# Moving normalised rows and inverse-softmax products from VectorE to GpSimd, with a new pace table, in a four-layer attention and MLP kernel

## The chip, the cores and the metric

The kernel runs on one core of a Trainium2 chip. The metric is the device time of one execution in microseconds (us). The core has TensorE (PE, matrix products), VectorE (DVE), ScalarE (ACT), GpSimd (POOL) and SyncE (SP, which issues the DMAs here). The profile adds PEld, TensorE's weight loads.

## The reference

Two layers of attention and two of a squared-ReLU MLP follow each other, on 2048 rows of 448 columns in bfloat16. Both attention layers use the same weights, and so do both MLPs.

```python
def A(x, wqkv, wo):                  # 16 heads of 28
    q, k, v = split(x @ wqkv)
    p = softmax(q @ k.T * 28 ** -0.5)
    return (p @ v).merge_heads() @ wo

def B(x, w1, b1, w2, b2):            # 448 -> 1792 -> 448
    r = maximum(x @ w1 + b1, 0)
    return (r * r) @ w2 + b2

x = x + A(layernorm(x)); x = x + B(layernorm(x), ...)
x = x + A(layernorm(x)); x = x + B(layernorm(x), ...)
```

`layernorm` is (x - mean) / sqrt(var + 1e-5), without weights.

## The kernel before

**Who orders the work.** The order of instructions on every engine is written by a planner in the kernel file when the program is built. Each piece of work is an `Op` with an engine, an assumed duration, what it depends on and which buffers it takes and gives back. Streams of Ops have priorities; `Planner.run` takes the Op that can start earliest, and by priority among equals. `Planner.earliest` works that time out from the ends of the dependencies (plus a latency of each engine, and `lat` of the Op) and from the engine's clock. An Op with `port=True` is on VectorE or GpSimd and uses SBUF on both sides; the planner doesn't start it inside such an Op of the other engine. Only the order is kept from the plan: on the chip each engine runs its list in order and waits on semaphores.

**Attention.** A score bank is 128 keys by 512 columns (two blocks of 128 keys for 256 queries of one head; for the last row blocks four for 128). A step computes three banks in one PSUM tile `sc` (`s_stream`, L924), and there are two such tiles. ScalarE takes the exponential of three banks in one instruction of 1536 columns (`e_stream`, L954), or of two banks in one of 1024 columns. In the second case VectorE does the third bank with an approximation of 2^x from bits, in four instructions: `take` (L1002, VectorE, reads PSUM and frees the bank), `part` (L1019, GpSimd, an add and a multiply on SBUF), `bend` (L1025, VectorE, a square) and `close` (L1032, VectorE, adds and writes bits). The function `apart` decides for each step whether VectorE takes a bank. One of its conditions is a bound on VectorE's planned backlog, read from the table `PACE` at the place of the step in the whole run:

```python
if max(0.0, pl.clock["DVE"] - now) + left[0] > PACE[i * len(PACE) // len(units)]:
    return None
```

The probabilities times V (`p_stream`, L1095) go into PSUM tiles `oT`, with the softmax sums in an extra column of each head. `p_stream` copies them to SBUF (L1121, L1123). For each pair of head groups `norm_pair` sends the sums to DRAM and back by three kinds of DMA on SyncE's queue (`dn`, `scr`, `rec`; L1198, L1209, L1217) with a reciprocal in between (L1203), so that their inverses lie spread over the rows, and multiplies (`mul`, L1222, 128x512, two float32 inputs and a bfloat16 output `oTn`). The last few row blocks use `norm_turn` with transposes on VectorE in its place (L1164 to L1180).

**The dense parts.** `chain` takes one block of 256 rows (128 at the end): the projection `wo` and the addition to `x_sb` (L655, L1231), statistics (L509, L514), `layernorm`, w1 with relu (L1289) and square (L1296), w2 and the addition, and in the first layer pair the statistics, `layernorm` and `qkv` for the second. `layernorm` takes the inverse root of the variance on GpSimd (L536, L537), normalises each 128 rows of 448 columns (`norm`, L619, into `xn`), transposes on TensorE (L559) and copies back (L571). In the opening the first three blocks are marked `early`. The very last block is done by `ends_last`.

**Fillers.** While the scores' share of TensorE is low, score matmuls are issued again (`again` in `s_stream`, into the same place), and `heat` issues products that nobody reads (L1516).

Of the kernel before, what the change touches and what calls it, by code (L numbers as in the profile page):

```python
# [13 lines left out]
ALU = mybir.AluOpType  # L14
# [12 lines left out]
GY = 0.65  # L27
# [48 lines left out]
PACE = (3.6, 2.2, 2.2, 1.8, 1.8, 1.8, 1.8, 3.0, 0.3, 0.9, 2.2, 2.2, 2.2, 1.4, 1.4, 1.4, 1.4, 1.4, 1.4, 2.2, 2.2, 2.2, 2.2, 1.4, 3.0, 3.0, 2.2, 2.2, 2.2, 1.8, 4.5, 4.5, 2.6, 2.6, 3.0, 3.0, 3.0, 3.6, 3.0, 1.4, 3.0, 4.5, 4.5, 4.5, 1.4, 1.4, 0.9, 1.4, 0.3, 1.4, 1.4, 1.4, 2.2, 2.2, 1.8, 1.8, 1.8, 1.8, 2.6, 2.6, 1.8, 1.8, 0.3, 6.0)  # L76
# [47 lines left out]
class Op:  # L124
    __slots__ = ("eng", "dur", "fn", "deps", "acq", "rel", "mode", "sets", "start", "end", "res", "turn", "ready", "lat", "need", "got", "more", "room", "port")

    def __init__(self, eng, dur, fn, deps=(), acq=None, rel=None, mode="full", sets=(), lat=0.0, need=1, port=False):
        self.eng = eng if isinstance(eng, tuple) else (eng,)
        self.dur, self.fn, self.deps, self.mode, self.lat = dur, fn, deps, mode, lat
        self.rel = rel if isinstance(rel, list) else ([] if rel is None else [rel])  # L130
        self.acq = acq if isinstance(acq, tuple) or callable(acq) else (() if acq is None else (acq,))
        self.sets = sets if isinstance(sets, list) else ([sets] if sets else [])
        self.start = self.end = self.res = self.turn = None
        self.need, self.got, self.more, self.port = need, [], 0.0, port
# [5 lines left out]
class Planner:  # L140
# [22 lines left out]
    def earliest(self, o):  # L163
        t = 0.0
        for d in o.deps:
            if not isinstance(d, Op):
                d = self.tok.get(d)
            if d is None or d.end is None:
                return None, None
            same = d.eng[0] == o.eng[0] and len(o.eng) == 1  # L170
            t = max(t, d.end + d.lat + ((0.03 if same else 0.10) if d.eng[0] == "DVE" else
                                (0.0 if same and d.eng[0] != "DMA" else LAT[d.eng[0]])))
# [68 lines left out]
def kernel(  # L241
# [12 lines left out]
    nc = tc.nc  # L254
# [265 lines left out]
    def layernorm(t0, nt, deps_of, early=False, mv=None, place=None, x_in=None, parts=False):  # L520
# [9 lines left out]
        for a, b in [(0, 1), (1, 2)] if single else [(0, nt)]:  # L530
# [9 lines left out]
            pl.spawn(EV, iter([rs]))  # L540
        box = {}
# [68 lines left out]
        for p0 in range(0, nt, wide):  # L610
# [4 lines left out]
            for j in js:  # L615
                xn = xns[2 * (own.turn % 2) + j % 2]

                def norm(e, j=j, xn=xn):
                    nc.vector.tensor_scalar(out=xn[:, 0:D], in0=x_sb[:, t0 + j, :],  # L619
                                            scalar1=mv[0][:, j, 0:1], scalar2=ln[j],  # L620
                                            op0=ALU.subtract, op1=ALU.mult)
                nm = Op("DVE", 0.39, norm, deps=[rss[j], *([] if x_in is None else [x_in])], sets=[("n", t0, j)] if early else (), port=True)
                yield nm
                xs.append((xn, nm))
# [387 lines left out]
    def a_rest(gi, c, box, unit):  # L1012
# [7 lines left out]
        y = Op("POOL", GY, part, deps=[c, ("p", gi)] if own else [c], acq=None if own else lambda: pd_free(unit), port=True)  # L1020
# [13 lines left out]
        o = Op("DVE", 0.683, close, deps=[h], rel=c, sets=("x", gi), port=True)  # L1034
# [151 lines left out]
    def norm_pair(l, qb, g, pair):  # L1186
# [34 lines left out]
        def mul(e):  # L1221
            nc.vector.tensor_tensor(out=oTn_of[l, qb][0][:, g:g + 2, 0:n], in0=both,  # L1222
                                    in1=box["r"][:, :, 0:n], op=ALU.mult)
        m = Op("DVE", 0.13 + 2 * n / 930, mul, deps=[r, oTn_of[l, qb][1]], rel=pair["own"], port=True)
# [9 lines left out]
    def chain(l, qb):  # L1234
# [43 lines left out]
        for f0 in range(0, NFC, pack):  # L1278
# [11 lines left out]
            def square(e, b=b, w=w, f0=f0):  # L1290
                r = b["r"][:, 0:w].rearrange("p (f q) -> p f q", q=n)
                b["h"] = h = hidden(f0 // pack)
                if e == "ACT":
# [4 lines left out]
            def then(o, b=b, square=square):  # L1298
                aside = not s_left and (l, qb) == (1, len(blocks[1]) - 2)
                b["s"] = Op("ACT" if aside else "DVE", 0.5 if aside else 0.42, square, deps=[o], rel=o, port=True)  # L1300
# [267 lines left out]
```

## Time and profile before

| | |
|---|---|
| median of 3 runs | 847.54 us (846.21 to 848.14) |
| profiled execution | 845.42 us |
| its span on the core | 843.6 us |
| mean granted clock of TensorE | 0.994 |
| busy: PE, DVE, ACT, POOL | 806.6, 783.8, 821.3, 225.3 us |
| exponentials L954 (1536 and 1024 columns) | 422 and 261 |
| banks of VectorE (L1002) | 260 |

The span runs from the first to the last instruction of the core; the time of the execution has 1.8 us more around it. Durations in the profile are those of single instructions, which overlap at their ends, so a busy time is less than count times mean. A "group by form" shows a line of the source, the engine, the operation, tiles and shapes, then the count, the busy time and mean duration, and the idle time of the engine before these instructions with what ended it. The table by stretches has the busy time of each engine with its count of instructions, then TensorE's granted clock and the DMA's share and rate. "A <- B: t, n, m" among the waits says that the engine waited in A for B, t us in all, n times, at most m. An answer on a line gives its count and the minimum, median and maximum duration in ns.

### The profile page before, as it was taken

Reading aid. Unit: us, or ns where it says so; the run is one execution under the profiler, and the core shown is the slowest. Engines: PE = TensorE matmul, PEld = TensorE weight load, DVE = VectorE, ACT = ScalarE, POOL = GpSimd, SP = SyncE. Lnnn points to the kernel's source line nnn. Section 1 sums busy time; section 2 is a strip of 40 time slices with the busy share of each in tenths; the row PEclk is TensorE's granted clock in tenths of the full one; section 3 lists DMA queues with packets and bytes.
Section 4 is the critical chain, followed back from the end, with each engine's and each line's share of the span. In section 5 each row is a group of like instructions: output and inputs, shape, how many; then the busy total and the mean of one; then the engine's idle time right before and its main releaser. Section 6 shows DMA issues by size and latency. Waiting matters only on the chain.

```text
span 843.6 us, 28341 instructions
## 1 busy us (share of the span) xinstructions
PE 806.6 (96%) x12255; PEld 428.6 (51%) x12255; DVE 783.8 (93%) x1610; ACT 821.3 (97%) x700; POOL 225.3 (27%) x354
## 2 busy tenths in 40 slices
PE   8999999999999999999999999989999999999997
PEld 4455545554545455455445444534554545545565
DVE  7999989999989999999999999989989999999955
ACT  8998999999999999999999999989999999999994
POOL 3222322223222233222332333332222222232300
PEclk9999999999999999999999999989999999999999
DMA  9200000000000000000000000011000000000000
GB/s 251 68 3 2 25 20 15 16 15 15 15 3 16 15 15 16 7 11 15 2 2 3 2 2 3 11 30 32 18 23 21 20 26 15 14 25 16 17 11 18
DMA packets 32365, 17.98 MB, mean 21 GB/s; under 512 B 17833, under 2 KB 31787, under 8 KB 32240
## 3 DMA queue, kind: packets, MB, share of 16 engines
q1 hardware_dynamic: 32240, 16.18, 6.9%
q8 instruction: 95, 1.56, 0.8%
q14 instruction: 30, 0.25, 0.1%
HBM read 13.88 MB, written 2.07 MB: 19 GB/s over the span
## 4 chain that ended last, share of the span: by engine, by line
PE 44%; DVE 27%; ACT 22%; issue 5%; DMA 1%; POOL 0%; SPq 0%; ACTq 0%; DVEq 0%
ACT pt L954 22%; PE mt L655 18%; PE sc L924 15%; PE oT L1095 8%; DVE v_w L1002 3%; DVE pt L1032 2%; DVE r L1289 2%; DVE V_sb L1032 2%; DVE K_sb L1002 2%; DVE pt L1025 2%; DVE V_sb L1025 1%; PE mt L1516 1%; DVE xn L619 1%; DVE oTn L1222 1%; DVE Q_sb L674 1%
## 5 line engine op out<-in xcount | busy, mean ns | idle before, releaser
L954 ACT ACTIVATE pt<-sc 128x1536 bf16<-128x1536 f32 (+1 forms) x683 | 810.0, 1377 | 9.1 <-PE sc L924 8.0
L924 PE MATMUL sc<-Q_sb,K_sb 32*128 32x256 bf16 (+1 forms) x5258 | 308.6, 267 | 22.3 <-ACT pt L954 17.1
L924 PEld LDWEIGHTS <-K_sb 32*128 32x128 bf16 x5258 | 131.1, 92 | 202.5 <-issue 157.5
L1095 PE MATMUL oT<-pt,V_sb 128*32 128x256 bf16 (+1 forms) x4008 | 154.2, 270 | 1.2 <-DVE pt L1032 0.7
L1002 DVE TENSOR_SCALAR v_w<-sc 128x512 f32<-128x512 f32 x187 | 127.4, 683 | 10.7 <-PE sc L924 9.9
L655 PE MATMUL mt<-xnT,w 128*128 128x256 bf16 (+1 forms) x888 | 118.6, 271 | 0.9 <-DVE xnT L571 0.4
L1095 PEld LDWEIGHTS <-V_sb 128*32 128x32 bf16 x4352 | 91.4, 96 | 50.9 <-issue 47.7
L655 PEld LDWEIGHTS <-w 128*128 128x128 bf16 x896 | 74.9, 98 | 35.6 <-issue 27.3
L1019 POOL TENSOR_SCALAR V_sb<-v_w 128x512 bf16<-128x512 uint16 x74 | 54.2, 733 | 131.1 <-DVE v_w L1002 130.3
L1289 DVE TENSOR_SCALAR r<-mt 128x512 bf16<-128x512 f32 x108 | 73.9, 684 | 6.3 <-PE mt L655 5.9
L1019 POOL TENSOR_SCALAR pt<-v_w 128x512 bf16<-128x512 uint16 x69 | 46.2, 670 | 114.0 <-DVE v_w L1002 91.4
L655 PE MATMUL mt<-w,V_sb 128*128 128x448 bf16 (+1 forms) x288 | 70.5, 349 | 0.0
L1002 DVE TENSOR_SCALAR K_sb<-sc 128x512 f32<-128x512 f32 x73 | 49.8, 683 | 4.6 <-PE sc L924 4.5
L1032 DVE SCALAR_TENSOR_TENSOR V_sb<-v_w,V_sb 128x512 int16<-128x512 f32 x74 | 51.5, 698 | 0.1
L1032 DVE SCALAR_TENSOR_TENSOR pt<-v_w,pt 128x512 int16<-128x512 f32 x69 | 47.7, 694 | 0.1
L1231 DVE TENSOR_TENSOR x_sb<-x_sb,mt 128x448 bf16<-128x448 bf16 x62 | 37.9, 612 | 8.7 <-PE mt L655 8.4
L1025 DVE TENSOR_TENSOR pt<-pt 128x512 bf16<-128x512 bf16 x99 | 45.1, 468 | 0.7 <-POOL pt L1019 0.7
L1025 DVE TENSOR_TENSOR V_sb<-V_sb 128x512 bf16<-128x512 bf16 x89 | 41.4, 474 | 2.5 <-POOL V_sb L1019 2.5
L1019 POOL TENSOR_SCALAR pt<-K_sb 128x512 bf16<-128x512 uint16 x30 | 21.6, 719 | 71.9 <-DVE K_sb L1002 51.5
L509 DVE BATCH_NORM_STATS2 st<-x_sb 128x6 f32<-128x448 bf16 x63 | 38.7, 616 | 1.2 <-DMA x_sb<-in_A_x_dram 0.7
L1516 PE MATMUL mt<-xn,ident 128*128 128x448 bf16 x105 | 36.5, 364 | 0.9 <-DVE oT_sb L1123 0.3
L655 PEld LDWEIGHTS <-V_sb 128*128 128x128 bf16 x302 | 24.3, 98 | 25.2 <-issue 12.1
(143 smaller groups left out, 882.1 us busy)
## 6 DMA issues: line engine op xcount, KB each, us to landing
rec<-scr SPq DMA_DIRECT2D x54, 128.0 KB
x_sb<-in_A_x_dram SPq DMA_DIRECT2D x8, 224.0 KB
out_dram<-x_sb SPq DMA_DIRECT2D x15, 112.0 KB
w<-in_B_w_dram SPq DMA_DIRECT2D x1, 1568.0 KB
w<-in_B_w_dram SPq DMA_DIRECT2D x1, 1344.0 KB
dn<-oT_sb SPq DMA_DIRECT2D x54, 4.0 KB
V_sb<-in_A_wqkv_dram SPq DMA_DIRECT2D x4, 168.0 KB
scr<-dn SPq DMA_DIRECT2D x27, 8.0 KB
```

The source lines that it names most:

```text
L509: nc.vector.bn_stats(out=box["st"][:, :], in_=x_sb[:, t0 + j, :] if src is None else src())
L655: nc.tensor.matmul(box["t"][:, c0:c0 + n], lhsT=lhsT() if callable(lhsT) else lhsT, rhs=rhs, start=a, stop=b)
L924: nc.tensor.matmul(dst[k][:, i * nt * P:(i + 1) * nt * P], lhsT=K_sb[l][rows, g, (kb + i) * P:(kb + i + 1) * P], rhs=Q_sb[rows, g, t0 * P: ...
L954: t = nc.scalar.activation(out=pt[:, 0:n], in_=gbuf[gi]["sc"][:, 0:n], func=AF.Exp, scale=float(np.log(2.0)) * 2.0 ** -FRAC)
L1002: t = nc.vector.tensor_scalar(out=box["w"], in0=two(src), scalar1=EXP_SHIFT, scalar2=EXP_LOW, op0=ALU.add, op1=ALU.max)
L1019: nc.gpsimd.tensor_scalar(out=two(pd), in0=low, scalar1=-EXP_MID * 65536, scalar2=EXP_BEND, op0=ALU.add, op1=ALU.mult)
L1025: nc.vector.tensor_tensor(out=pd, in0=pd, in1=pd, op=ALU.mult)
L1032: nc.vector.scalar_tensor_tensor(out=two(pd.bitcast(DT.int16)), in0=box["w"], scalar=EXP_BITS, in1=two(pd), op0=ALU.add, op1=ALU.add)
L1095: nc.tensor.matmul(box["t"][DHP * hh:DHP * hh + DHP, 0:n], lhsT=V_sb[l][:, kb + i, 4 * g + hh, :], rhs=p[:, c0:c0 + n], start=begin and kb ...
L1231: nc.vector.tensor_tensor(out=x_sb[:, tb, lo:hi], in0=x_sb[:, tb, lo:hi], in1=t[:, 0:hi - lo], op=ALU.add)
L1289: nc.vector.tensor_scalar(out=r[:, 0:w], in0=t[:, 0:w], scalar1=0.0, scalar2=None, op0=ALU.max)
L1516: nc.tensor.matmul(t[:, 0:D], lhsT=ident[:, :], rhs=xns[0][:, 0:D], start=True, stop=True)
```

## The change

Four things are changed.

1. The normalisation of `layernorm` runs on GpSimd, but not in the `early` blocks. It is written as (x + (-mean)) * rstd there; the new `turned` negates the means on VectorE, one instruction of 128x2 (or 128x1) per call, into spare columns of the same small tile.
2. The product `mul` of `norm_pair` runs on GpSimd.
3. `PACE` has 128 entries in place of 64, from 1.0 to 4.0 with a mean of 2.41 (before 0.3 to 6.0, mean 2.23). Its lines are left out below.
4. Assumed durations and latencies of the planner change: `GY`, the new `YL` and `XL`, `GN` and `GM`. `earliest` keeps the dependencies' part of its result in `base`; it gives the same.

Squares on GpSimd are written in too, but switched off (`GS_ON = 0`).

```diff
-GY = 0.65
+GY = 0.617
+XL = 0.25
+YL = 0.05
+GN = 0.56
+GM = 1.3
+GS = 1.3
+GN_E = 0
+GM_ON = 1
+GS_ON = 0
+GS_STOP = 100
...
             rs = Op("POOL", 0.95, rsqrt, deps=[mv[1][b - 1]], sets=[("rs", t0 + a)] if early else (), port=True)
             rss += [rs] * (b - a)
             pl.spawn(EV, iter([rs]))
+            if not parts and (GN_E or not early):
+                def turned(e, a=a, b=b):
+                    ln["m"] = mv[0][:, 2:4, 0]
+                    nc.vector.tensor_scalar(out=ln["m"][:, a:b], in0=mv[0][:, a:b, 0], scalar1=-1.0, scalar2=None, op0=ALU.mult)
+                ng = Op("DVE", 0.07, turned, deps=[mv[1][b - 1]])
+                yield ng
...
                 def norm(e, j=j, xn=xn):
+                    if e == "POOL":
+                        nc.gpsimd.tensor_scalar(out=xn[:, 0:D], in0=x_sb[:, t0 + j, :],
+                                                scalar1=ln["m"][:, j:j + 1], scalar2=ln[j],
+                                                op0=ALU.add, op1=ALU.mult)
+                        return
                     nc.vector.tensor_scalar(out=xn[:, 0:D], in0=x_sb[:, t0 + j, :],
                                             scalar1=mv[0][:, j, 0:1], scalar2=ln[j],
                                             op0=ALU.subtract, op1=ALU.mult)
-                nm = Op("DVE", 0.39, norm, deps=[rss[j], ...
+                on = GN_E or not early
+                nm = Op("POOL" if on else "DVE", GN if on else 0.39, norm, deps=[rss[j], ...
...
-        y = Op("POOL", GY, part, deps=..., acq=..., port=True)
+        y = Op("POOL", GY, part, deps=..., acq=..., port=True, lat=YL)
...
-        o = Op("DVE", 0.683, close, deps=[h], rel=c, sets=("x", gi), port=True)
+        o = Op("DVE", 0.683, close, deps=[h], rel=c, sets=("x", gi), port=True, lat=XL)
...
         def mul(e):
-            nc.vector.tensor_tensor(out=oTn_of[l, qb][0][:, g:g + 2, 0:n], in0=both,
+            (nc.gpsimd if e == "POOL" else nc.vector).tensor_tensor(out=oTn_of[l, qb][0][:, g:g + 2, 0:n], in0=both,
                                     in1=box["r"][:, :, 0:n], op=ALU.mult)
-        m = Op("DVE", 0.13 + 2 * n / 930, mul, deps=[r, oTn_of[l, qb][1]], rel=pair["own"], port=True)
+        m = Op("POOL" if GM_ON else "DVE", GM if GM_ON else 0.13 + 2 * n / 930, mul, deps=[r, oTn_of[l, qb][1]], rel=pair["own"], port=True)
```

38 lines of the change are left out of this document (22 added, 16 removed).

## The prediction

> **What bounds the kernel now.** I read the page first, for the share of each engine:
>
> ```profile
> span 843.6 us, 28341 instructions
> PE 806.6 (96%) x12255; PEld 428.6 (51%) x12255; DVE 783.8 (93%) x1610; ACT 821.3 (97%) x700; POOL 225.3 (27%) x354
> PE 44%; DVE 27%; ACT 22%; issue 5%; DMA 1%; POOL 0%; SPq 0%; ACTq 0%; DVEq 0%
> ```
>
> Three engines are above 90%, and the chain of waits is shared among them, so shares alone don't say which one sets the time. TensorE's is the least firm: the kernel fills its gaps with repeated scores and the junk products of L1516. So I took the table by stretches, cut at the first and the last exponential (10.65 and 829.2 us), with three odd stretches beside:
>
> ```profile
> core 0: us, PE busy (x) PEld busy (x) DVE busy (x) ACT busy (x) POOL busy (x), PEclk, DMA share, GB/s
> 75.00:80.00 5.00, 4.41 (x65) 2.88 (x67) 4.74 (x11) 2.25 (x2) 0.62 (x1) 1.00 0.02 5
> 398.30:443.70 45.40, 43.47 (x651) 21.91 (x640) 44.40 (x96) 45.40 (x42) 15.64 (x25) 1.00 0.01 2
> 545.00:560.00 15.00, 13.19 (x186) 5.24 (x182) 12.34 (x27) 13.17 (x12) 4.78 (x6) 0.66 0.13 37
> 10.65:829.20 818.55, 787.46 (x12073) 416.10 (x12070) 769.50 (x1556) 810.03 (x684) 219.10 (x338) 0.99 0.07 19
> 829.20:843.60 14.40, 10.72 (x133) 7.82 (x130) 7.56 (x26) 3.08 (x7) 0.56 (x1) 1.00 0.06 18
> ```
>
> Between the first and the last exponential ScalarE is busy 810.03 of 818.55 us, 99%. That stretch is a queue of exponentials; the 14.4 us behind it are TensorE's. Then the groups by form, and ScalarE's waits:
>
> ```profile
> L954 ACT ACTIVATE pt<-sc 128x1536 bf16<-128x1536 f32 x422 | 607.8, 1541 | 4.7 <-PE sc L924 4.0 <-PE oT L1095 0.3
> L954 ACT ACTIVATE pt<-sc 128x1024 bf16<-128x1024 f32 x261 | 278.7, 1113 | 4.4 <-PE sc L924 4.0 <-ACT pt L954 0.3
> ACT pt L954 <- PE sc L924: 8.0, 12, 3.1
> L1002 DVE TENSOR_SCALAR v_w<-sc 128x512 f32<-128x512 f32 x187 | 127.4, 683 | 10.7 <-PE sc L924 9.9
> L619 DVE TENSOR_SCALAR xn<-x_sb,mv,rstd 128x448 bf16<-128x448 bf16 x63 | 26.0, 437 | 2.6 <-POOL rstd L537 2.6
> L1222 DVE TENSOR_TENSOR oTn<-oT_sb,rec 128x512 bf16<-128x512 f32 x27 | 21.8, 806 | 1.3 <-DMA rec<-scr 1.3
> ```
>
> There are 683 steps of three score banks. In 422 ScalarE takes all three, in 261 two, and VectorE takes the third (L1002). Consecutive exponentials overlap by their last 0.2 us, so the price is start to start: the median in the trace is 1.330 us for three banks and 0.904 for two. 422 x 1.330 + 261 x 0.904 = 797.2 us of the 818.6; the other 21 are small delays. A bank moved to VectorE is worth 1.330 - 0.904 = 0.426 us.
>
> **The change, part by part.** The changed program can be built, and its order of instructions counted. The steps stay 683, and now 403 are of three banks and 280 of two, so VectorE takes 279 banks in place of 260. On ScalarE: 19 x 0.426 = **-8.1 us**, on the path, as long as its delays stay what they are.
>
> What VectorE gains and pays, by busy time over count. Each bank costs it L1002 0.682, L1025 0.468 and L1032 0.699: 19 x 1.849 = +35.1. Away go 57 of the 63 normalisations (57 x 0.413 = -23.5; the six of the opening stay) and all 28 products (27 x 0.807 + 0.4 = -22.2). The negated mean is new, 29 of at most 0.15 us (the 128x1 rows L1404 and L1414 take 0.153 and 0.148): +4.3. One relu and one square go to ScalarE behind its last exponential: -1.1. Sum -7.4: VectorE is lent more than it pays.
>
> GpSimd gets 19 more L1019 (0.707 each, +13.4), the 57 normalisations and the 28 products. No row shows the last two there. L1019 has one input of 512 columns and takes 0.617 us when alone and up to 1.256:
>
> ```profile
> L1019 POOL TENSOR_SCALAR pt<-K_sb x30: 617/618/1256, 145.1 to 765.2; 128x512 bf16<-128x512 uint16 x30
> L1222 DVE TENSOR_TENSOR oTn<-oT_sb,rec x28: 416/684/1100, 101.6 to 804.3; 128x512 bf16<-128x512 f32 x27, 128x256 bf16<-128x256 f32 x1
> ```
>
> A normalisation of 448 columns lies between 0.617 x 448/512 = 0.54 and 1.26 us; I take 0.6, by the row that is alone. A product reads two inputs: between 0.62 and twice that behind a wait of 0.68, 1.9; I take 1.2. That is 57 x 0.6 + 28 x 1.2 + 13.4 = 81 us, and GpSimd goes from 225 to about 307, 37%: its own room is ample. Each result comes 0.2 to 0.5 us later than VectorE's. Transposes wait for the one, the projection for the other; TensorE sat 0.9 us in all behind L619 and 0.5 behind L1222, with other work in between, so this is covered; uncovered, 57 x 0.2 + 28 x 0.5 would be 25 us. The product now waits for its broadcast (rec) at the head of GpSimd's queue, with L1019 behind it, and VectorE's L1025 behind those. On VectorE that wait came once, 1.3 us: the transfers land in time. SyncE's issues keep their order but for neighbours in the opening, at nothing.
>
> The two engines disturb each other, though. Of the 260 L1025, 166 ran beside no GpSimd instruction, at 0.415 us on average, and 94 did, at 0.568; for L1032 173 at 0.680 and 87 at 0.743; for L1222 14 at 0.663 and 14 at 0.921; with L619 and L1296 this costs VectorE 28.4 us. 6.4 of it leave with the moved work. GpSimd's undisturbed work on SBUF goes from 260 x 0.617 + 35 = 196 us to 279 x 0.617 + 35 + 34 + 34 = 275, so the remaining 22 grow by 275/196 and by 6% for more VectorE instructions, to 33. VectorE's gain of 7.4 turns into a loss of 2 to 4. Within the exponentials it then has about 772 us of work in 810, 95%. The stretch 398.3 to 443.7 held 98% with ScalarE never idle, so it still fits. I charge **+1 us** of delays (from 0 to +8).
>
> Here a page speaks against the change. By the Trainium skill's page "SBUF — State Buffer", section "SBUF: two separate sides", the port pair that VectorE and GpSimd share is locked for a whole instruction, and the later one waits it out. The longest cases agree: an L1025 of 0.834 us is 0.415 and 0.42 more. By that rule the 664 two-input instructions of VectorE, 0.82 per us, meet the new 34 + 34 us on GpSimd 56 times, and wait half a product (0.6) or half a normalisation (0.3): 25 us in place of the 11 by the rows. VectorE is then at 786 us, 97%, just below what that stretch held; the delays go to their upper end, 8, and the sum to 850.0. That counts with the first rival.
>
> Two places differ in TensorE's order. From 75.4 to 79.8 us it has 52 matmuls for projections and outputs between two score tiles, held by VectorE's evictions; ScalarE waits 3.1 us. In the changed order the longest such run has 28 (some 2 us of work), with three of that kind: **-2.0** (between 0 and -3.1). The tail gets longer. After the last scores the program before has 24 matmuls of w1 with 128 columns, 15 of w2 with 448 and 32 of outputs; the changed one has 40, 33 and 64. At the tail's rates (0.056, 0.189 and 0.013 us): 0.9 + 3.4 + 0.4 = 4.7, and the last addition has 448 columns in place of 128, +0.26. TensorE is busy 12.6 of the 13.5 us there, so little idle time is left to take it: **+4.6** (from +3.8 to +5.5). In the main stretch this work lay under the exponentials, so nothing comes back for it.
>
> Sum: -8.1 + 1.0 - 2.0 + 4.6 = **-4.5 us**. The profiled execution took 845.42 (span 843.6 and 1.8 around it), 2.1 below the median of 847.54; the difference carries over: **843.0 us**.
>
> **Rivals.** *VectorE falls behind through the shared access to SBUF*, slower. It counts from the point where VectorE's work passes 98% of the shortened stretch, 0.98 x 811 = 795, that is 23 us more disturbance than I counted. By the growth above, 49% of the 558 L1025 and L1032 will be hit (181 of 520 now). A hit costs them 0.110 on average now; at the 0.258 that L1222 pays, the disturbance is 73 us and not 33: 772 + 40 = 812 needs 828 us at 98%, 17 over: 843.0 - 1 + 17 = 859. At 0.225 a hit it would be 851, and below 0.19 VectorE keeps up. For it: VectorE stands above 95% in the stretch shown, and the instructions that GpSimd newly gets are as long as VectorE's own, or longer. Against: the mean price of a hit now is less than half of that, and ScalarE waited 8 us in all for late scores. Chance 0.24.
>
> *Nothing measurable*: the tail takes 5.5, the stall at 80 us comes back elsewhere and one more stretch at a low clock (545 to 560, granted 0.66, some 2.5 us lost) appears, which fewer repeated scores (5116 L924 in place of 5258, of which 4352 are needed) make likelier: -8.1 + 5.5 + 2.5 = 0, 847.5. Chance 0.13.
>
> *The small delays shrink too*: the low-clock stretch doesn't come back (-2.5) and the new pace leaves VectorE less crowded where ScalarE now waits, -4 more: 836.5 to 839. Chance 0.1. That the change doesn't do what it says is out: the order has 57 normalisations and 28 products on GpSimd and 280 narrow exponentials.
>
> **How the numbers follow.** The forecast has 0.53 and spans 839.5 to 845.8 by its bounds. A measurement here tells 0.2%, 1.7 us, from no change. Faster: 0.53 + 0.1 = 0.63; same 0.13; slower 0.24. The range takes in the third rival but for its end and the nearer half of the first: 836.5 to 852, leaving out some 0.04 below and 0.13 above.
>
> **What would show it.** Right: L954 near 802 us with 403 and 280; an idle time before it of 6 to 10 us; VectorE at 93 to 95%; the last exponential ends near 819, and 18 to 19 us follow. Wrong: L1025 and L1032 far above 0.47 and 0.70; a product over 1.9 us on GpSimd; ScalarE's waits for L924 well above 8 us; or a tail like before's.

## The result, and the profile after

The changed kernel takes 856.6 us (854.97 to 857.06, 4 runs), the kernel before 847.83 us beside it on the same chip (846.21 to 848.14, 4 runs): a ratio of 1.0104 [1.0085, 1.0123]. It is 1% slower; 843.0 was forecast, and 836.5 to 852 as range. The profiled execution took 856.41 us.

The profile's page:

```profile
span 854.4 us, 28257 instructions
PE 806.0 (94%) x12126; PEld 423.8 (50%) x12126; DVE 795.5 (93%) x1609; ACT 817.1 (96%) x702; POOL 324.4 (38%) x458
DVE 40%; PE 36%; ACT 15%; issue 7%; POOL 1%; DMA 0%; POOLq 0%; ACTq 0%; DVEq 0%
```

In the last line, the shares of the chain that ended last, VectorE has risen from 27% to 40%; its busy share has not moved from 93%. The table by stretches, cut again at the first and the last exponential, with one stretch inside (columns as in the prediction's table):

```profile
10.77:835.11 824.34, 781.87 (x11896) 407.82 (x11893) 779.73 (x1552) 804.82 (x683) 318.51 (x443) 0.99 0.07 18
835.11:854.40 19.29, 15.56 (x181) 11.18 (x178) 9.08 (x29) 4.11 (x9) 0.56 (x1) 0.97 0.08 25
158.30:206.80 48.50, 45.45 (x700) 23.75 (x696) 47.84 (x92) 47.17 (x41) 23.22 (x30) 1.00 0.04 8
```

The exponentials are the 403 and 280 that were counted: 403 x 1.330 + 280 x 0.904 = 789.1 us, 8.1 less than before. But they now lie in 824.3 us. The delays between them have gone from 21.4 to 35.2 us, and the tail from 14.4 to 19.3. So the span's +10.8 is -8.1, +13.8 and +4.9, and 0.2 from rounding and the opening. The delays show as ScalarE waiting for scores, and as TensorE waiting for VectorE to read a score bank:

```profile
ACT pt L978 <- PE sc L948: 18.0, 30, 1.8
PEld L948 <- DVE v_w L1026: 21.0, 47, 1.5
POOL oTn L1246 <- DMA rec<-scr: 13.6, 10, 3.5
```

Before, ScalarE's wait was 8.0 us in 12 places, the longest 3.1. Now it is 30 short waits. The third line is new: the product waits at the head of GpSimd's queue for its broadcast. (Lines move by the edit: scores L948, exponentials L978, `take` L1026, `part` L1043, `bend` L1049, `close` L1056, `norm` L638, `mul` L1246.) The two instructions that moved, by an answer on their lines, and one of VectorE's groups by form:

```profile
L1246 POOL TENSOR_TENSOR oTn<-oT_sb,rec x28: 727/1272/1702, 103.0 to 810.0; 128x512 bf16<-128x512 f32 x27, 128x256 bf16<-128x256 f32 x1
L638 POOL TENSOR_SCALAR xn<-x_sb,mv,rstd x57: 712/718/1395, 18.6 to 817.6; 128x448 bf16<-128x448 bf16 x57
L1049 DVE TENSOR_TENSOR V_sb<-V_sb 128x512 bf16<-128x512 bf16 x89 | 45.8, 527 | 1.5 <-POOL V_sb L1043 1.5
```

On GpSimd the product takes 1.27 us as median (1.31 as mean) and the normalisation 0.72 (0.83 as mean). This group of `bend`s took 474 ns on average before and takes 527 now. What one product does to the rest is read from the timeline (start, duration, engine, line; the bracket is the idle time before and what ended it):

```profile
693.67 1.27 POOL L1246 TENSOR_TENSOR oTn<-oT_sb,rec 128x512 bf16<-128x512 f32 x1 [1.02 <-DMA rec<-scr]
693.76 1.72 DVE L1056 SCALAR_TENSOR_TENSOR pd<-K_sb,pd 128x512 int16<-128x512 f32 x1
...
695.41 0.83 DVE L1049 TENSOR_TENSOR h<-h 128x512 bf16<-128x512 bf16 x1
696.16 0.41 DVE L1145 COPY oT_sb<-oT 128x256 f32<-128x256 f32 x1
696.49 0.68 DVE L1026 TENSOR_SCALAR v_w<-sc 128x512 f32<-128x512 f32 x1
696.62 0.60 PE L679 MATMUL mt<-xnT,w 128*128 128x256 bf16 x4 [1.15 <-DVE oT_sb L1145]
...
697.15 0.40 PE L948 MATMUL sc<-Q_sb,K_sb 32*128 32x256 bf16 x6
...
697.65 2.79 ACT L978 ACTIVATE pt<-sc 128x1536 bf16<-128x1536 f32 x2 [0.88 <-PE sc L948]
```

The product starts 0.09 us ahead of a `close`. That `close` takes 1.72 us instead of 0.68. Behind it in VectorE's order stand a `bend`, an eviction of `oT` (its copy to SBUF) and a `take`; TensorE idles 1.15 us for the eviction, its next scores come late, and ScalarE idles 0.88 us. The `close` ends 0.55 us after the product. That holds for all nine `close`s that begin inside a product, whenever they began; the seven `bend`s that begin at least 0.3 us before a product's end all end 0.28 us after it.

To compare kernels I went through the instructions of each trace and took, for every `bend`, `close` and square that overlaps a GpSimd instruction, its duration beyond the undisturbed one (0.411 us for `bend` and squares, 0.678 for `close`). I call the sum VectorE's **stand**: 22.4 us before, 45.0 after. The larger part of the new 22.6 us is the product's. In 16 meetings with a `bend` or a `close` in which the product began first, VectorE stood 0.86 us on average and 1.08 at most, 13.8 us in all. Where VectorE began first it lost nothing (9 meetings, at most 0.02 us). A `part` that began first cost a `bend` 0.32 and at most 0.42 us, the same as before, but there are more such meetings: with squares the `part`s' share rose by 6.8 us. A normalisation that began first cost 0.09 on average in 15 meetings, 1.3 us in all.

A part of the longer delays lies elsewhere. Cut at the changes of TensorE's granted clock, the changed kernel has these two stretches at 0.50 within the exponentials:

```profile
546.20:559.80 13.60, 13.18 (x147) 5.16 (x147) 9.31 (x21) 11.03 (x10) 4.80 (x7) 0.50 0.15 42
785.10:788.50 3.40, 3.40 (x34) 1.66 (x33) 2.60 (x6) 2.43 (x3) 0.00 (x0) 0.50 0.00 0
```

and the kernel before these:

```profile
545.70:552.50 6.80, 6.29 (x80) 2.26 (x72) 4.78 (x12) 5.66 (x5) 1.34 (x2) 0.50 0.15 42
555.90:559.30 3.40, 3.40 (x40) 0.98 (x34) 3.40 (x8) 3.16 (x3) 1.44 (x2) 0.50 0.19 64
```

That is 17 us in place of 10 in the profiled executions, and ScalarE's delays in and at the ends of these stretches are 5.9 us against 2.9. So some 3 of the 13.8 us go with the clock. Whether the product brought the lower clock on isn't shown.

### The profile page after: what moved, and what is told of

Read it like the earlier page. It is cut to its first block, busy times and chain, and to the rows that moved or that the text cites. A ratio compares the mean times of both kernels' runs of the same rounds, so it can differ in the third digit from the quotient of the medians.

```text
span 854.4 us, 28257 instructions
## 1 busy us (share of the span) xinstructions
PE 806.0 (94%) x12126; PEld 423.8 (50%) x12126; DVE 795.5 (93%) x1609; ACT 817.1 (96%) x702; POOL 324.4 (38%) x458
## 4 chain that ended last, share of the span: by engine, by line
DVE 40%; PE 36%; ACT 15%; issue 7%; POOL 1%; DMA 0%; POOLq 0%; ACTq 0%; DVEq 0%
ACT pt L978 15%; PE mt L679 15%; PE sc L948 12%; DVE v_w L1026 6%; PE oT L1119 6%; DVE pt L1056 4%; DVE r L1313 3%; DVE V_sb L1056 3%; DVE pt L1049 3%; DVE V_sb L1049 2%; DVE K_sb L1026 2%; DVE h L1056 2%; PE mt L1543 2%; DVE V_sb L1322 1%; DVE pd L1056 1%
## 5 line engine op out<-in xcount | busy, mean ns | idle before, releaser
L978 ACT ACTIVATE pt<-sc 128x1536 bf16<-128x1536 f32 (+1 forms) x683 | 804.8, 1347 | 20.1 <-PE sc L948 18.0
L948 PE MATMUL sc<-Q_sb,K_sb 32*128 32x256 bf16 (+1 forms) x5116 | 302.7, 267 | 28.2 <-ACT pt L978 17.9
L948 PEld LDWEIGHTS <-K_sb 32*128 32x128 bf16 x5116 | 123.4, 92 | 210.8 <-issue 152.5
L1026 DVE TENSOR_SCALAR v_w<-sc 128x512 f32<-128x512 f32 x200 | 135.4, 681 | 11.0 <-PE sc L948 10.6
L1043 POOL TENSOR_SCALAR pt<-v_w 128x512 bf16<-128x512 uint16 x81 | 57.5, 710 | 98.6 <-DVE v_w L1026 73.5
L1043 POOL TENSOR_SCALAR V_sb<-v_w 128x512 bf16<-128x512 uint16 x70 | 49.4, 705 | 109.8 <-DVE v_w L1026 108.9
L1026 DVE TENSOR_SCALAR K_sb<-sc 128x512 f32<-128x512 f32 x79 | 53.6, 680 | 4.6 <-PE sc L948 4.1
L1056 DVE SCALAR_TENSOR_TENSOR pt<-v_w,pt 128x512 int16<-128x512 f32 x81 | 57.8, 720 | 0.1
L1049 DVE TENSOR_TENSOR pt<-pt 128x512 bf16<-128x512 bf16 x121 | 54.7, 466 | 0.0
L638 POOL TENSOR_SCALAR xn<-x_sb,mv,rstd 128x448 bf16<-128x448 bf16 x57 | 47.2, 834 | 14.5 <-DVE mv L556 6.1
L1056 DVE SCALAR_TENSOR_TENSOR V_sb<-v_w,V_sb 128x512 int16<-128x512 f32 x70 | 50.9, 728 | 0.1
L1049 DVE TENSOR_TENSOR V_sb<-V_sb 128x512 bf16<-128x512 bf16 x89 | 45.8, 527 | 1.5 <-POOL V_sb L1043 1.5
L1246 POOL TENSOR_TENSOR oTn<-oT_sb,rec 128x512 bf16<-128x512 f32 (+1 forms) x28 | 36.7, 1309 | 18.7 <-DMA rec<-scr 13.6
L1043 POOL TENSOR_SCALAR pt<-K_sb 128x512 bf16<-128x512 uint16 x40 | 27.9, 698 | 41.0 <-DVE K_sb L1026 27.4
```

Source lines behind the costliest of these rows:

```text
L638: nc.gpsimd.tensor_scalar(out=xn[:, 0:D], in0=x_sb[:, t0 + j, :], scalar1=ln["m"][:, j:j + 1], scalar2=ln[j], op0=ALU.add, op1=ALU.mult)
L948: nc.tensor.matmul(dst[k][:, i * nt * P:(i + 1) * nt * P], lhsT=K_sb[l][rows, g, (kb + i) * P:(kb + i + 1) * P], rhs=Q_sb[rows, g, t0 * P: ...
L978: t = nc.scalar.activation(out=pt[:, 0:n], in_=gbuf[gi]["sc"][:, 0:n], func=AF.Exp, scale=float(np.log(2.0)) * 2.0 ** -FRAC)
L1026: t = nc.vector.tensor_scalar(out=box["w"], in0=two(src), scalar1=EXP_SHIFT, scalar2=EXP_LOW, op0=ALU.add, op1=ALU.max)
L1043: nc.gpsimd.tensor_scalar(out=two(pd), in0=low, scalar1=-EXP_MID * 65536, scalar2=EXP_BEND, op0=ALU.add, op1=ALU.mult)
L1049: nc.vector.tensor_tensor(out=pd, in0=pd, in1=pd, op=ALU.mult)
```

## Experiments in the changed order

The theories: (A) the product and the normalisation make VectorE stand, and the stand at the head of its queue is passed on to TensorE and ScalarE; (B) the product's wait for `rec` holds up GpSimd's queue, with the `part`s behind it, and so VectorE; (C) the order itself, made with the new table, gives VectorE banks where it has no room; beside them the longer tail. The planner's assumed durations stay in these kernels, so that every engine has the changed kernel's order, and only the instruction itself differs.

**No wait for the broadcast.** The product takes the same tile twice.

```diff
-                                    in1=box["r"][:, :, 0:n], op=ALU.mult)
+                                    in1=both, op=ALU.mult)
```

> The order of the changed program is kept, instruction for instruction; the product on GpSimd multiplies oT_sb by itself, so that it no longer waits for the broadcast rec (this leaves the division by the softmax sums out). Theory A, the two engines hold each other up at SBUF: the product keeps its 1.27 us, nothing changes, 855 to 857 us, delays of the exponentials some 35 us as in the changed kernel. Theory B, GpSimd's queue stands behind the product while rec is under way (13.6 us, 10 times): these waits go, the delays fall by 4 to 6 us, 850 to 852. Theory C, the order itself (the new table and assumed costs) gives VectorE banks where it has no room: 855 to 857.

Measured: 851.33 us, 1.0052 [1.0034, 1.007]. The edit took away the wait and shortened the product as well, so by itself it doesn't tell A from B:

```profile
L1246 POOL TENSOR_TENSOR oTn<-oT_sb 128x512 bf16<-128x512 f32 x27 | 29.6, 1097 | 1.8
```

Its 16 meetings cost 0.62 us on average, and at most 0.88 of a product that mostly takes 1.04. The stand is 41.0 us.

**A memset in place of the product.**

```diff
-            (nc.gpsimd if e == "POOL" else nc.vector).tensor_tensor(out=oTn_of[l, qb][0][:, g:g + 2, 0:n], in0=both,
-                                    in1=box["r"][:, :, 0:n], op=ALU.mult)
+            nc.gpsimd.memset(oTn_of[l, qb][0][:, g:g + 2, 0:n], 0.5)
```

> Same order; the product is a memset of the same output on GpSimd, which reads nothing from SBUF (this leaves the product out). Theory A: the 28 long two-input instructions stop holding VectorE; the L1049 and L1056 that ran beside them lose some 10 us, the delays of the exponentials fall by 4 to 7, 849 to 852. Theory B: as in the run without the wait, 850 to 852. Theory C: 855 to 857.

Measured: 845.01 us, 0.9975 [0.9963, 0.9987]. That is below all that was expected. It is 2.1 us faster than the kernel before; the sum -8.1 + 1.3 + 4.9 of the lines below gives -1.9. ScalarE's wait and the stretches:

```profile
ACT pt L978 <- PE sc L948: 9.5, 16, 1.8
L1246 POOL MEMSET oTn<- 128x512 bf16 x27 | 14.2, 524 | 1.3
12.25:824.00 811.75, 778.39 (x11896) 408.54 (x11893) 765.67 (x1552) 802.14 (x683) 293.88 (x441) 0.99 0.07 18
824.00:843.30 19.30, 15.58 (x181) 11.19 (x179) 9.09 (x29) 4.12 (x9) 0.56 (x1) 1.00 0.08 25
```

The exponentials have 811.75 us here, 22.7 of them delays, 1.3 more than before: the +1 of the forecast. So the order alone (C) doesn't make the kernel slow. The tail is as long as the changed kernel's. The stand falls to 30.0 us; the memset's own meetings cost at most 0.01 us.

This kernel has the same 683 steps, narrow and wide ones in the same places, so its delays can be set against the changed kernel's step by step. Of the 12.8 us by which they differ, start to start, 9.3 lie in the 100 steps that begin from 1 us before to 6 us after one of the 18 stands behind a product, 2.8 in the low-clock stretches (10.2 us long here), and 0.7 in the other 568 steps.

**A short normalisation**, of 32 columns in place of 448, the product as in the changed kernel; then both at once.

```diff
-                        nc.gpsimd.tensor_scalar(out=xn[:, 0:D], in0=x_sb[:, t0 + j, :],
+                        nc.gpsimd.tensor_scalar(out=xn[:, 0:32], in0=x_sb[:, t0 + j, 0:32],
```

> Same order; the 57 normalisations on GpSimd write 32 of their 448 columns (the others keep what an earlier block left there), some 0.2 us in place of 0.72. Theory A: 57 x 0.5 = 28 us less on the shared access, the delays fall by 3 to 6, 850 to 853. Theories B and C: 855 to 857.

> Same order; both of the last two edits. GpSimd's load is back near that of before, with the changed order, its 280 narrow exponentials and its longer tail. Theory A: the delays are back near 21 us, so 848.5 from the exponentials and the tail: 789 + 21 + 10.8 + 19.3 = 840 of span, 842 to 846 us. Theory B: 850 to 852. Theory C: 855 to 857.

Measured: 851.39 us, 1.0049 [1.003, 1.0069], for the short normalisation; 844.87 us, 0.9975 [0.9963, 0.9988], for both. With the product there, halving the normalisation (0.37 us in place of 0.72) is worth 5 us; without it, nothing. The stands are 40.8 and 28.2 us.

**One input in place of two.** The product is replaced by a multiplication of `oT_sb` by a constant, without `rec`.

```diff
-            (nc.gpsimd if e == "POOL" else nc.vector).tensor_tensor(out=oTn_of[l, qb][0][:, g:g + 2, 0:n], in0=both,
-                                    in1=box["r"][:, :, 0:n], op=ALU.mult)
+            nc.gpsimd.tensor_scalar(out=oTn_of[l, qb][0][:, g:g + 2, 0:n], in0=both, scalar1=0.02, scalar2=None, op0=ALU.mult)
```

> The changed kernel's order; the product on GpSimd is a multiply of oT_sb by a constant: one input of 512 columns, no wait for rec (the division by the softmax sums is left out). It stands between the two-input product without the wait (1.04 us, 851.3) and the memset (0.52 us, 845.0). If the length of GpSimd's hold on SBUF is what counts, it takes some 0.62 us and comes to 846 to 847; if reading SBUF at all is what counts, 849 to 851, with the L1049 and L1056 that meet it above those of the memset.

Measured: 847.9 us, 1.0017 [0.9999, 1.0036].

```profile
L1246 POOL TENSOR_SCALAR oTn<-oT_sb 128x512 bf16<-128x512 f32 x27 | 41.9, 1553 | 2.1
ACT pt L978 <- PE sc L948: 9.4, 15, 1.8
```

The instruction was expected at some 0.62 us. It is longer than the product, 1.55 against 1.33 us as means of the 512-column ones, and meets VectorE more often: 34 meetings in which it began first. They cost 0.11 us on average and at most 0.42. Often VectorE's instruction ended while GpSimd's still ran, by up to 0.61 us, which no `bend` or `close` inside a product did. So it is not how long GpSimd is busy; it is that the product reads two inputs.

**The wait alone.** A product of two columns waits for `rec`, and a memset does the rest.

```diff
-            (nc.gpsimd if e == "POOL" else nc.vector).tensor_tensor(out=oTn_of[l, qb][0][:, g:g + 2, 0:n], in0=both,
-                                    in1=box["r"][:, :, 0:n], op=ALU.mult)
+            o = oTn_of[l, qb][0]
+            nc.gpsimd.tensor_tensor(out=o[:, g:g + 2, 0:1], in0=both[:, :, 0:1], in1=box["r"][:, :, 0:1], op=ALU.mult)
+            nc.gpsimd.memset(o[:, g:g + 2, 0:n], 0.5)
```

> The changed kernel's order; on GpSimd a product of two columns that waits for rec, and then the memset (the product is left out but for these columns, which the memset overwrites). It adds the wait alone to the memset (845.0). If the standing of GpSimd's queue behind rec costs the 4.4 us that the run without the wait gained: 849 to 850. If the wait cost only together with the long product behind it: 845 to 847.

Measured: 845.73 us, 0.9982 [0.9964, 1.0001], against 0.9975 [0.9963, 0.9987] for the memset without a wait.

```profile
L1247 POOL TENSOR_TENSOR oTn<-oT_sb,rec 128x2 bf16<-128x2 f32 x28 | 7.5, 267 | 19.1 <-DMA rec<-scr 17.7
```

GpSimd waits 17.7 us for `rec` here, more than in the changed kernel, and the time hardly moves: the medians differ by 0.7 us, and the intervals overlap. Theory B falls as the cause of the 11 us.

**The product in four instructions** of 128 columns on GpSimd, and **the product on VectorE** at the same place of the order.

```diff
-            (nc.gpsimd if e == "POOL" else nc.vector).tensor_tensor(out=oTn_of[l, qb][0][:, g:g + 2, 0:n], in0=both,
-                                    in1=box["r"][:, :, 0:n], op=ALU.mult)
+            for i in range(2):
+                for lo in range(0, n, 128):
+                    nc.gpsimd.tensor_tensor(out=oTn_of[l, qb][0][:, g + i, lo:lo + 128], in0=both[:, i, lo:lo + 128],
+                                            in1=box["r"][:, i, lo:lo + 128], op=ALU.mult)
```

```diff
-            (nc.gpsimd if e == "POOL" else nc.vector).tensor_tensor(out=oTn_of[l, qb][0][:, g:g + 2, 0:n], in0=both,
+            nc.vector.tensor_tensor(out=oTn_of[l, qb][0][:, g:g + 2, 0:n], in0=both,
```

> The changed kernel's order and result; the product on GpSimd is done in four instructions of 128 columns in place of one of 512. Theory A, a VectorE instruction with two SBUF inputs that comes after the start of a two-input one on GpSimd stands until that one ends (16 such meetings cost 13.8 us in the changed kernel): each meeting now ends with a piece of some 0.4 us, 16 x 0.25 = 4 us, so 8 us less of delays: 847 to 850. If VectorE is held until all four are done: 855 to 858.

> The changed kernel's order and result; the product stands on VectorE at the place where the planner put it on GpSimd. Theory A: the 13.8 us of meetings go, but VectorE gets 27 x 0.81 + 0.4 = 22 us of work in places where the plan has none; if its delays pass on at the rate seen so far (about 0.8 us per us), -11 + 18: 861 to 864. If VectorE has room after all, since it is busy 95% between the first and last exponential: 847 to 852.

Measured: 850.42 us, 1.0038 [1.0023, 1.0053], in pieces; 854.02 us, 1.0076 [1.0048, 1.0104], on VectorE. The lines of the product, in pieces and on VectorE:

```profile
L1248 POOL TENSOR_TENSOR oTn<-oT_sb,rec 128x128 bf16<-128x128 f32 x110 | 58.5, 561 | 9.4 <-DMA rec<-scr 7.7
```

```profile
L1246 DVE TENSOR_TENSOR oTn<-oT_sb,rec 128x512 bf16<-128x512 f32 x27 | 19.6, 728 | 0.0
```

In pieces GpSimd works 58.5 us on the products instead of 36.7, and the kernel is faster by 6 us: 39 `bend`s, `close`s and squares that began while a piece ran lost 0.20 us on average and at most 0.27, 7.7 us in all against 14.2 with the whole product. Put back on VectorE, the product takes 20 us of it, and that is little better, if at all, than the whole product on GpSimd (the intervals overlap). That lies between the two ranges that were expected; it fits a VectorE that with 280 banks in this order has room for neither.

Put together, by VectorE's stand:

| kernel in the changed order | stand, us | time, us | ratio to before |
|---|---|---|---|
| changed | 45.0 | 856.6 | 1.0104 |
| one tile twice, no wait | 41.0 | 851.33 | 1.0052 |
| short normalisation | 40.8 | 851.39 | 1.0049 |
| four pieces | 38.1 | 850.42 | 1.0038 |
| one input | 34.2 | 847.9 | 1.0017 |
| memset | 30.0 | 845.01 | 0.9975 |
| two columns, then memset | 30.0 | 845.73 | 0.9982 |
| short normalisation and memset | 28.2 | 844.87 | 0.9975 |

Between the first and the memset, 15.0 us of stand carry 0.0129 x 847.5 = 10.9 us of time, 0.73 us for each us. The rest lie within 2 us of that line. It is a relation in this order, where VectorE has little room, and no constant of the chip. The clock is in it too. Within one kernel the runs spread with the granted clock: with one tile twice, from 850.91 us at 0.994 to 853.25 at 0.990, and some 0.5 us for each thousandth over all runs here. The changed kernel's runs have a median of 0.9885, the memset's 0.992, so by this estimate about 2 of the 10.9 us go with the clock. The rows with one tile twice and with the short normalisation have 0.993, so the same holds for their distance to the first.

## Experiments in the order of before

Here the planner's durations are those of the kernel before, and so are all orders, with 261 narrow exponentials; only the engine or the form of one operation changes.

**The product on GpSimd, whole and in four pieces** (the same two edits at L1222).

> The order, the table and the 261 narrow exponentials of the kernel before; only the product stands on GpSimd, whole. From the runs on the changed order: a microsecond that VectorE stands behind GpSimd costs 0.73, and one of VectorE's own work, by the run with the product on VectorE, some 0.4. VectorE loses 22 us of work (-8.5) and meets the product some 14 times at 0.85 (+9): 846 to 850. If the order and table of the changed kernel are what made the meetings: 839 to 843.

> As the run with the whole product, but in four pieces of 128 columns. Theory A: the meetings cost 4 to 5 us in place of 12: 840 to 845, that is 4 to 6 under the whole product. If VectorE's work is hidden anyway in the order before: within 2 us of the kernel before, 845 to 849.

Measured: 848.37 us, 1.0013 [1.0, 1.0027], whole; 846.99 us, 1.0000 [0.9986, 1.0013], in pieces.

```profile
L1222 POOL TENSOR_TENSOR oTn<-oT_sb,rec 128x512 bf16<-128x512 f32 x27 | 35.3, 1308 | 11.6 <-DMA rec<-scr 9.7
```

The whole product has 16 meetings with a `bend` or a `close` of 0.73 us on average here, and moving it from VectorE costs about 1 us. The same comparison in the changed order, the product on GpSimd against the product on VectorE, is 1.0104 against 1.0076, 2.4 us and not clear of noise; the 11 us above are those of a product against none, which wasn't run in this order. In pieces the stand is 5 us lower (30.5 against 35.8) and the time 1.4, and VectorE is 9.3 us less busy than before (774.5 against 783.8) without the kernel being faster. So in this order relief and stand either weigh little or cancel; these runs don't tell which. Theory A's gain for the pieces, 840 to 845, did not come.

**The 57 normalisations on GpSimd**, with the negated mean on VectorE; then with the product in pieces as well.

```diff
+                    if not early:
+                        if j == 0:
+                            ln["m"] = mv[0][:, 2:4, 0]
+                            nc.vector.tensor_scalar(out=ln["m"][:, 0:nt], in0=mv[0][:, 0:nt, 0], scalar1=-1.0, scalar2=None, op0=ALU.mult)
+                        nc.gpsimd.tensor_scalar(out=xn[:, 0:D], in0=x_sb[:, t0 + j, :],
+                                                scalar1=ln["m"][:, j:j + 1], scalar2=ln[j],
+                                                op0=ALU.add, op1=ALU.mult)
+                        return
```

> The order, table and 261 narrow exponentials of before; only the 57 normalisations stand on GpSimd, with the negated mean on VectorE. VectorE loses 20 us of work (-8); GpSimd's one-input instructions cost little where they are met, but the result comes 0.3 us later: 840 to 845. If VectorE's work is hidden anyway: 845 to 849. If the later result delays the transposes: 849 to 853.

> The order, table and 261 narrow exponentials of before, the normalisations and the product in four pieces on GpSimd. Theory A: the gains of both, VectorE 38 us lighter: 834 to 842. If VectorE's work is hidden anyway: 845 to 849.

Measured: 857.98 us, 1.0103 [1.0056, 1.0151], and 861.02 us, 1.0152 [1.0123, 1.018].

```profile
POOL xn L623 <- DVE mv L622: 28.1, 20, 5.0
PEld L559 <- POOL xn L623: 6.4, 9, 1.7
PE tp L559 <- POOL xn L623: 4.6, 8, 1.4
```

Both are slower than all that was expected. A normalisation meets VectorE cheaply, 0.08 us on average. Its price here is another one: the results come late, and in front of the transposes TensorE's weight loads wait 6.4 us and its matmuls 4.6 (the second and the third line). In the changed kernel, whose planner knows of the normalisation on GpSimd, these waits are 0.6 and 0.2 us. The granted clock is lower as well, 0.98 in the profiled execution against 0.994 before, and the four runs spread from 853.61 to 860.83 us, so a part of the 1.0% goes with the clock. In the old order the edit doesn't pay; with an order made for it these waits are nearly gone.

## Experiments planned anew, and the tail

**The product back on VectorE, and planned so** (`GM_ON = 0`, 274 narrow exponentials); the same with `GN = 0.72`, the measured duration of the normalisation; **both moved operations back** with the new table (275); and **both moved, with the old table** and `GY`, `XL`, `YL` of before (263).

```diff
-GM_ON = 1
+GM_ON = 0
```

```diff
-GM_ON = 1
+GM_ON = 0
-GN = 0.56
+GN = 0.72
```

```diff
-GM_ON = 1
+GM_ON = 0
...
-            if not parts and (GN_E or not early):
+            if False:
...
-                on = GN_E or not early
+                on = False
```

```diff
-GY = 0.617
-XL = 0.25
-YL = 0.05
-PACE = (2.2, 2.2, 2.2, 4.0, ...
+GY = 0.65
+XL = 0.0
+YL = 0.0
+PACE = (3.6, 2.2, 2.2, 1.8, ...
```

> The changed kernel with the product on VectorE again (GM_ON = 0); the planner makes a new order, with 274 narrow exponentials in place of 280, and the same 16.5 us of TensorE's work behind the last scores. If the product on GpSimd is the fault, by its hold on SBUF and its wait: -13 x 0.426 = -5.5 for the exponentials against before, +4.9 for the tail, delays at 22 to 28 us: 847 to 853. If the normalisation and the new order are at fault as well: 853 to 857.

> As the run with the product back on VectorE, and the planner is told 0.72 us for a normalisation on GpSimd, what the profile shows, and not 0.56; again 274 narrow exponentials. If wrong assumed durations make VectorE's banks late: 1 to 3 us below the run without this, 846 to 850. If not: within 1.5 us of it.

> The new table, assumed costs and latencies alone: normalisation and product on VectorE, a new order with 275 narrow exponentials. VectorE then has 15 x 1.849 = 28 us more than before. If the table asks for more banks than VectorE can take: 855 to 870, with ScalarE waiting for scores. If the new assumed costs make a better order: 842 to 847.

> Both moves to GpSimd with the table PACE, GY, XL and YL of before; a new order with 263 narrow exponentials, 3 more than before (-1.3 us), a tail of 16.1 in place of 11.8 us (+4.3). Theory A: meetings with the product cost about what they do in the changed kernel, 8 to 12 us: 857 to 862. If the new table is what makes meetings costly, because it leaves VectorE no room: 848 to 852.

Measured: 866.75 us, 1.0228 [1.019, 1.0266]; 861.46, 1.0171 [1.0141, 1.0201]; 868.49, 1.0247 [1.0217, 1.0276]; 868.23, 1.025 [1.0218, 1.0283]. ScalarE's waits in the first and the third:

```profile
ACT pt L978 <- PE sc L948: 27.8, 25, 11.8
```

```profile
ACT pt L978 <- PE sc L948: 28.5, 21, 15.0
```

All four have one wait of 11 to 15 us near the passage between the two layer pairs that neither of the two given kernels has. The planner gives a different order there for each set of its inputs. The first, the second and the last lie outside all ranges that were expected; the third lies within its 855 to 870, but with 15.0 of its 28.5 us of waits in that one stop. These runs therefore say that the table and the durations belong to one set of engines, and nothing on what a part of the change is worth. What the new table is worth by itself stays open.

**A shorter tail.** In the changed kernel, with the product in pieces, and in the kernel before, `norm_turn` is taken for all pairs of the last but one row block:

```diff
-QUICK = 2
+QUICK = 0
```

> The changed kernel with each product in four instructions of 128 columns on GpSimd (s1_four_pieces, 850.42 us) and, in the last but one row block of the second attention layer, norm_turn for all pairs of head groups (QUICK = 0 in place of 2). Planned with this, TensorE's order is the same up to its row 21865 of 24254; behind the last scores it has work of 7.6 us by the tail's rates in place of 16.5 of the changed kernel's whole stretch there. Still 280 narrow exponentials. Theory (the tail is a cost of its own, to be added to the stands): the tail goes from 19.3 us to about 14, the time to 844 to 848 us, at or below the kernel before. Rival (the tail's work only moves up under the exponentials and delays scores there): the last exponential ends 3 to 5 us later, the time stays at 849 to 851.

> The kernel before with QUICK = 0 alone, 261 narrow exponentials. TensorE has 12.7 us of work behind the last scores by the tail's rates in place of 11.8. Expected: 846 to 849 us, within 0.2% of the kernel before or slightly over. If it were faster by over 2 us, then what the other kernel gains would not be the removal of the changed order's longer tail, but norm_turn in that block by itself.

Measured: 857.09 us, 1.012 [1.0104, 1.0137], 6.7 over the pieces alone; 848.54 us, 1.0018 [1.0006, 1.0031], in the kernel before. Stretches and waits of the first:

```profile
10.57:838.95 828.38, 790.63 (x11991) 414.87 (x11988) 778.40 (x1566) 804.24 (x683) 336.50 (x523) 0.99 0.07 19
838.95:854.70 15.75, 9.25 (x109) 7.62 (x107) 7.03 (x25) 1.67 (x3) 0.56 (x1) 0.89 0.05 16
ACT pt L978 <- PE oT L1119: 9.3, 1, 9.3
```

The tail is 3.5 us shorter, and the stretch of exponentials 10 longer, by one stop of 9.3 us: at 821.6 us TensorE begins a run of w1 and w2 products of that block, which now lies ahead of the last probabilities times V, and ScalarE has no place for its next result. The rival's mechanism, work that moves up under the exponentials, is what the profile shows, and its size was too small (849 to 851): moved ahead, the work costs more than it did behind. Whether the tail can be cut for nothing by another order wasn't tried.

No kernel that computes the whole reference came out faster than the kernel before; with the product in pieces in its order it is the same (1.0000).

## Why the prediction was wrong

**What was right.** The exponentials: -8.1 us, exactly as counted. The tail: +4.6 forecast, +4.9 measured. The product's duration: 1.2 taken, 1.27 measured. The normalisation's was taken too short, 0.6 against 0.72 as median and 0.83 as mean, but within its bounds.

**The step that failed** is the term of +1 us of delays, and the reasoning under it: VectorE would be 95% busy within the exponentials, below the 98% at which one stretch still ran without a stop, "so it still fits". VectorE was 94.6% busy (779.7 of 824.3), and the delays grew by 13.8 us. Two things were wrong in it.

- *The size of a meeting.* The disturbance was put at 33 us by scaling the old mean with GpSimd's time, as though any microsecond of GpSimd were like a `part`. It was 45. Over all 26 overlaps with a `bend` or a `close`, those in which VectorE began first included, a product cost 0.53 us each, and 0.86 in the 16 that count, where the scaling took 0.110; that is because it reads two inputs: with one input a longer instruction cost 0.11 (847.9 us). The row that came nearest stood in the prediction, an L1025 that lost 0.42 to a `part`, but that is about the most that a one-input instruction took, however long.
- *The criterion.* An average over 811 us can't say whether a queue in order has room at a given place. In the stretch from 158.3 to 206.8 us VectorE is at 47.84 of 48.50, 98.6%, and delays are 2.9 us against 1.2 with the memset; and in the 40 steps from 539.7 us it is at 87%, and they are 5.8 against 2.9: 1.4 of this difference lie in the low-clock stretch, but the two products at 562.0 and 581.5 us are followed by 0.7 and 0.9. In the timeline above the stand lies just ahead of an eviction and a `take`, and is passed on at once, whatever the engine does later. The product's removal took 10.9 us off the time while VectorE's share within the exponentials only went from 94.6 to 94.3%.

**The first rival** had the mechanism and the wrong condition: it was to decide only above 98%, or 0.19 us a hit. Measured by its own count, 246 of 558 `bend` and `close` were hit (44%; it had 49%), at 0.163 us each: by its condition VectorE keeps up, which the average confirms, and the kernel is slower all the same. Its 859 lies near the result by way of a larger hit than there was. The rule of the Trainium skill, "SBUF — State Buffer", section "SBUF: two separate sides", by which the engine that begins first holds the shared ports for its whole instruction, described the product well (up to 1.08 of 1.27 us) and gave 25 us of stand in place of 11. That this is near the 22.6 that came is partly luck: it puts some 17 on the product and 8 on the normalisation, and the runs show 14, 2 and another 7 from more meetings with `part`. For one-input instructions the runs disagree with it: at most 0.42 us of 1.5. The 850.0 that went with it fell short because the delays were still capped at 8.

**The second rival** counted one more stretch at a low clock, 2.5 us. In part it came: the profiled execution has 17 us at a clock of 0.50 in place of 10, and some 3 us more of delays there. The rest of that rival didn't decide.

**The burst at 75 to 80 us** was to give 2.0 back. The stop of 3.1 us there did go (the longest wait is now 1.8), but the delays of the first 80 steps rose from 4.5 to 6.7 us, and with the memset they are 6.2: others of 1 to 2 us came in with the new order. That term was 2 us too good, whatever the product does.

**The waits for `rec`**, charged at nothing because "the transfers land in time": they don't, GpSimd waits 13.6 us for them, and still the price of nothing was right, as 845.73 against 845.01 shows. **The late normalisations** were covered, as forecast, but by the new order: in the old one they cost 1.0%, 8.7 us with the clock's part, within the 25 that the prediction gave for the uncovered case.

In sum: -8.1 and +4.9 are as forecast, and about +1.3 of delays belong to the new order and the normalisation, against -1.0 that was forecast for delays and burst together. The other 12.5 us of delays in the profiled executions, 10.9 in the medians, are gone when the product is a memset: some 9 of them lie at the product's meetings, 2 to 3 go with the lower clock. The forecast had neither.

## What to carry to other kernels

Before work is moved to GpSimd beside a busy VectorE, look at what it reads: an instruction with two SBUF inputs stopped VectorE's two-input work here for nearly its whole length (up to 1.08 of 1.27 us), and if it must go there, short pieces did better although they take longer in sum. An average share of 95% didn't tell whether an engine that works in order had room: ask which instruction stands behind the one that is stopped, and who waits for that. To find the price of a moved operation in a planned kernel, keep the order and change the instruction alone; planning anew changed too much here to tell. And look at the granted clock of both profiles before all of a difference is put down to the change.

## What was not expected of the hardware

- A one-input instruction of GpSimd costs a `bend` or `close` that comes after it at most 0.43 us in the kernel before and the changed one, and at most 0.47 in any kernel here, whether it takes 0.62, 0.72 or 1.50 us; a two-input one costs up to 0.88 of 1.04 and 1.08 of 1.27; a memset of 0.52 us costs nothing (at most 0.01).
- A two-input VectorE instruction that begins inside a two-input one of GpSimd, at least 0.3 us before its end, ends at a fixed time after it: 0.28 us for a `bend`, 0.55 for a `close`, in each of the 47 such meetings of the changed kernel, of the one with one tile twice, and of the whole product in the order of before.
- On GpSimd a 128x512 float32 tile times a constant (1.50 us) takes longer than the product of two such tiles (1.27), and the product of a tile with itself takes 1.04. Four pieces of 128 columns take 0.56 each on average, 2.2 in sum.
- A disturbed two-input instruction loses its time only when GpSimd began first. When VectorE began first, the mean excess was 0.04 us or less beside the whole product, the normalisation and `part` in the changed kernel.
